# Sinkhorn attention followed by a routed expert layer: the first-layer tile's second bank no longer ordered behind the first bank's relu, the attention's exponential issued a unit earlier, expert pieces ahead of the placing, the ranking spread over the Sinkhorn rounds and GpSimd

## The chip, the cores and the metric

The kernel runs on one core of a Trainium2 chip. The metric is device time in microseconds (us) for one launch. A core has five engines, each of which takes its own instructions in order: TensorE (PE, with PEld for its weight loads), VectorE (DVE), ScalarE (ACT), GpSimd (POOL) and SyncE (SP); semaphores order them among each other, and DMA queues move data beside them. TensorE's results go to PSUM, from where ScalarE or VectorE copy them to SBUF (an "eviction").

## The reference, cut to what matters

```python
def _attn_ref(q, k, v, sort_net):            # (4, 8, 768, 64), 8 blocks of 96
    P = sort_net                             # (4, 8, 8, 8)
    for _ in range(5):
        P = np.exp(P - np.max(P, axis=-1, keepdims=True))
        P = P / (np.sum(P, axis=-1, keepdims=True) + 1e-09)
        P = P / (np.sum(P, axis=-2, keepdims=True) + 1e-09)
    k_sorted = einsum('bhij,bhjcd->bhicd', P, k_b)    # the same for v
    attn = softmax(scale * q_b @ k_sb.T)     # inside each block of 96
    return attn @ v_sb

def _moe_ref(x, modality_id, w_gate, modality_bias, w1, w2):   # x: 3072 x 512
    logits = x @ w_gate + modality_bias[modality_id]
    e_idx = np.argmax(logits, axis=1)        # one of 8 experts for each row
    gate_w = softmax(logits)[row, e_idx]
    out[mask] = gate_w * (np.maximum(x[mask] @ w1[e], 0) @ w2[e])
```

The rows of x are the attention's output, heads side by side. The kernel assumes that each of the two modalities sends its rows to one expert, the one that its bias prefers, checks that on the chip, and has a slow path that recomputes everything where it does not hold. The slow path does not run with this data.

## The kernel before, in words

**Start.** GpSimd issues the loads of `v`, `k`, `q` (halves of the batch: g = 0, 1) and fills constants. Five Sinkhorn rounds (L224 to L242) alternate one exponential on ScalarE with five small VectorE operations; TensorE meanwhile runs 28 matmuls on the identity (`spin`). Then `make_bd` turns P into a block matrix, `rank_a` to `rank_e` compute for each row its place among the rows of its modality (`m_` the modality bits, `cumz` running counts, `dest` the row's place within a block's window, `off` the window's offset, `eI` the two experts), on VectorE and TensorE. `load_w` reads `eI` into a register and issues the experts' weights; they go to two homes, wA and wB. `sort_v` (8 chunks, tiles `va`) and `sort_k` (6 chunks, tiles `ka`) mix the blocks by P; each chunk is evicted by ScalarE or VectorE, as `pick` decides from running sums of estimated cost. `prep_q` transposes q (tiles `tq`).

**Units.** There are 32 units, one for a pair of batches, a block and half of the heads: `scores(u)` (8 matmuls, tile `sc`), `expo(u)` (one exponential, 96x768, on ScalarE into `attnT[u % 2]`), `av(u)` (8 matmuls, tile `op`, then a reciprocal and a multiplication on VectorE into `xb`). Two units make a pair of blocks, and `place(t)` multiplies its 2 x 96 rows by the permutation `perm` into tile `pm` (10 matmuls) and copies them into the window of `XT` that `off` names: two copies on ScalarE for an even pair, on VectorE for an odd one. Rows of modality 0 gather from the front of `XT`, rows of modality 1 from its end.

**Slots and pieces.** `SLOTS` (L60) cuts `XT` into stretches of 128 or 256 rows, each with a home of weights and the number of pairs that have to be placed first. A slot is worked off in pieces: the gate `mG` (tile `lg`), the first layer `mL1` (tile `hp`, two PSUM banks, 4096 matmul columns; each bank is evicted by its own `relu` into `hT`), the second layer `mL2` (tile `yp`, 4096 columns, one eviction into `y` and one scattering DMA to `out`). `run_pieces(n)` takes the next n pieces whose slot's pairs are placed. There are 25 pieces of each layer.

**Order.** A manual schedule keeps every engine's instructions in the order in which the code emits them. PSUM tiles with two banks (`sc`, `op`, `pm`, `hp`, `va`, `ka`, `rk`) come from a pool of three, in turn, so that the fourth waits until the first has been evicted; `tq`, `lg` and `yp` come from a pool of two single banks. `do_unit` is the period of the units:

```python
def do_unit(u, last, n):
    expo(u)
    if u < last:
        scores(u + 1)
    if u % 2 == 0 and pending:
        do_place()
    run_pieces(n)
    av(u)
```

Units 0 to 6 of the first half run no pieces. Between the halves stand `sort_v(1)` and `sort_k(1)` with one piece behind each chunk, then eight `prep_q`. What is left of the pieces runs after the last unit; ahead of the last slot's second layer a check of the assumption runs on VectorE, and its one matmul (`gp`) stands in TensorE's order.

Of the kernel before, what the change touches and what calls it, by code (L numbers as in the profile page):

```python
# [24 lines left out]
def kernel(  # L25
# [15 lines left out]
    NB = 8  # L41
# [18 lines left out]
    SLOTS = [("A", 0, 256, 3), ("A", 256, 256, 6), ("B", 0, 256, 3), ("B", 256, 256, 6),  # L60
# [41 lines left out]
    v_in = singles.tile([128, 128, D], BF16)  # L102
# [84 lines left out]
    nc.gpsimd.memset(v_in[:, BLK:].rearrange("p c d -> p (c d)").bitcast(U32), 0)  # L187
# [8 lines left out]
    idm = singles.tile([BLK, 32, 128], BF16)  # L196
    nc.gpsimd.memset(idm.bitcast(U32), 0)
# [4 lines left out]
    nc.gpsimd.tensor_copy(idm[:, :, 0:2].rearrange("p o z -> p z o"), idI)  # L202
# [3 lines left out]
    nc.gpsimd.memset(XT[:, :, PAD0:CAP - PAD0].bitcast(U32), 0)  # L206
# [14 lines left out]
    for _ in range(28):  # L221
        nc.tensor.matmul(spin[:, 0].rearrange("p (a b) -> p a b", a=4), ident, id4, start=True, stop=True)

    for it in range(5):  # L224
# [4 lines left out]
        if it == 0:  # L229
            nc.vector.tensor_reduce(jmask, id3s, AX.X, ALU.add)  # L230
        elif it == 1:
            nc.vector.tensor_reduce(bmask, id3, AX.X, ALU.add)
        elif it < 4:
            nc.vector.tensor_copy(sel[it - 2], ident[0:BH, (it - 2) * 16:(it - 1) * 16].broadcast_to([BH, 16, NB]))
# [23 lines left out]
    def sort_v(g, ch):  # L258
        acc = ps(f"va{g}_{ch}").rearrange("p b (z x) -> p (b z) x", x=128)
        for z in range(8):  # L260
            nc.tensor.matmul(acc[:, z], v_in[:, :, ch * 8 + z], bd[g], start=True, stop=True)  # L261
        evac(v_sb[0:BLK, :, ch * 8:(ch + 1) * 8], acc[0:BLK].rearrange("p z x -> p x z"), 1024)
# [24 lines left out]
    st = {}  # L287

    def small(name, n, dt=FP32, rows=128):
        return singles.tile([rows, n], dt, tag=name, name=name)  # L290

    def rank_a():
        mbf = singles.tile([32, 3, 32], BF16)
        nc.vector.tensor_copy(mbf, modI[:, :, 0].rearrange("p (r t) -> p t r", t=3))
        mp = ps1("mp", BF16)[0:BLK, 0:32]
        nc.tensor.transpose(mp, mbf.rearrange("p t r -> p (t r)"), ident[0:32, 0:32])
        m_ = st["m"] = small("m_", 32, BF16, BLK)
        nc.vector.tensor_copy(m_.rearrange("p (g i r) -> p g i r", g=2, i=8),
                              mp.rearrange("p (g r i) -> p g i r", g=2, r=2))
        ci = st["ci"] = small("ci", 32, BF16, BLK)  # L300
        nc.vector.tensor_tensor_scan(ci, ones_bf[0:BLK, 0:32], m_, 0.0, ALU.mult, ALU.add)

    def rank_b():
        rk = st["rk"] = ps("rk")
        nc.tensor.matmul(rk[:, 1, 0:32], ones_bf[0:BLK], st["ci"], start=True, stop=True)
        nc.tensor.matmul(rk[:, 0, 0:32], maskUT[0:BLK], st["m"], start=True, stop=True)
        nc.vector.tensor_copy(cumz[:, 1:33], rk[:, 1, 0:32])
        f_ = st["f"] = small("f_", 1)
        nc.vector.tensor_scalar(f_, cumz[:, 32:33], float(HALF), None, ALU.is_le)
        d_ = small("d_", E)  # L310
        nc.vector.tensor_tensor(d_, bias2[:, 1], bias2[:, 0], ALU.subtract)
        bAB = st["bAB"] = singles.tile([128, 2, E], FP32, tag="bAB", name="bAB")
        nc.vector.scalar_tensor_tensor(bAB[:, 0], d_, f_, bias2[:, 0], ALU.mult, ALU.add)
        nc.vector.scalar_tensor_tensor(d_, d_, f_, bias2[:, 1], ALU.mult, ALU.subtract)
        nc.vector.tensor_scalar(bAB[:, 1], d_, -1.0, None, ALU.mult)
# [14 lines left out]
    def rank_ok():  # L330
        nm = st["nm"] = small("nm", 32)
        nc.vector.tensor_tensor(nm, cumz[:, 1:33], cumz[:, 0:32], ALU.subtract)
        w_ = small("w_", 33)
        nc.vector.tensor_tensor(w_, cumz, mid, ALU.subtract)
        dv = small("dv", 64)
        nc.vector.tensor_tensor(dv[:, 0:32], w_[:, 1:33], w_[:, 1:33], ALU.mult)
        nc.vector.tensor_scalar(dv[:, 32:64], nm, float(BLK // 2), None, ALU.subtract)
        nc.vector.tensor_tensor(dv[:, 32:64], dv[:, 32:64], dv[:, 32:64], ALU.mult)
        nc.vector.tensor_tensor(dv, dv, marg, ALU.is_le)
        good = st["good"] = small("good", 1)  # L340
        nc.vector.tensor_reduce(good, dv, AX.X, ALU.min)
# [540 lines left out]
```

## Time and profile before

| | |
|---|---|
| median of 3 runs | 258.31 us (257.79 to 259.61) |
| the profiled execution's own time | 259.06 us |
| its span in the trace | 257.3 us |
| TensorE matmul busy | 183.6 us (71%) |
| VectorE busy | 109.7 us (43%) |
| ScalarE busy | 93.3 us (36%) |
| GpSimd busy | 58.6 us (23%) |
| mean granted TensorE clock | 0.839 of 2.4 GHz |

The granted clock has two levels, 1.2 and 2.4 GHz (0.5 and 1.0 in the rows); a mean between them says for what share of a stretch each was granted. Matmul ends are modelled, so the step from one start to the next says more about a matmul's cost than the duration of a single row does.

### The profile page before, as it was taken

How to read it: one execution, taken by the hardware profiler on the slowest of the kernel's cores; microseconds unless marked ns; L12 is line 12 of the kernel's file. 1: busy time of each engine (PE TensorE's matmuls, PEld its weight loads, DVE VectorE, ACT ScalarE, POOL GpSimd, SP SyncE). 2: the span in 40 equal slices, each digit the busy share in tenths (PEclk: the TensorE clock that was granted, in tenths of full speed). 3: DMA queues.
4: the chain of work that ended last, by engine and by line, in shares of the span. 5: the costliest groups of instructions: out<-in, count | busy, mean ns of one | idle time of the engine just before them, and what ended most of it. 6: DMA issues, size and time to landing. Idle time of an engine off the chain costs nothing. (4 is left out here: it accounts for less than half of the span.)

```text
span 257.3 us, 5170 instructions
## 1 busy us (share of the span) xinstructions
PE 183.6 (71%) x2166; PEld 127.6 (50%) x2183; DVE 109.7 (43%) x294; ACT 93.3 (36%) x141; POOL 58.6 (23%) x102
## 2 busy tenths in 40 slices
PE   4756886568658778888987567676778747878581
PEld 1345765446435456676565345553555534555240
DVE  4878877750453272323435433325234460022411
ACT  2124466323632534334346414334434503433030
POOL 7877332100000157111310001011011111123013
PEclk9956675557855899999999659799799997999889
DMA  5999999998000119811111001011011110212101
GB/s 69 199 214 197 207 197 209 212 214 179 3 1 3 41 45 166 160 41 43 43 43 43 0 3 41 3 41 41 3 41 43 41 41 0 84 42 83 44 33 55
DMA packets 16460, 20.36 MB, mean 79 GB/s; under 512 B 9999, under 2 KB 12079, under 8 KB 16432
## 3 DMA queue, kind: packets, MB, share of 16 engines
q0 software_dynamic: 15664, 19.93, 39.0%
q8 instruction: 18, 0.29, 0.5%
q1 hardware_dynamic: 768, 0.06, 0.3%
q14 instruction: 10, 0.08, 0.1%
HBM read 27.32 MB, written 6.55 MB: 132 GB/s over the span
## 5 line engine op out<-in xcount | busy, mean ns | idle before, releaser
L547 POOL DMA_INDIRECT out_dram<-y,ids x25 | 24.5, 979 | 174.5 <-ACT y L544 131.3
L528 PE MATMUL hp<-XT,wA 128*128 128x256 bf16 (+1 forms) x224 | 32.7, 305 | 8.8 <-ACT hT L516 6.5
L528 PE MATMUL hp<-XT,wB 128*128 128x256 bf16 (+1 forms) x224 | 28.2, 272 | 11.5 <-ACT hT L516 6.1
L516 ACT ACTIVATE hT<-hp 128x512 bf16<-128x512 f32 x34 | 20.2, 595 | 36.7 <-PE hp L528 36.6
L539 PEld LDWEIGHTS <-hT 128*128 128x128 bf16 x200 | 19.4, 102 | 24.2 <-issue 6.7
L528 PEld LDWEIGHTS <-wA 128*128 128x128 bf16 x224 | 22.2, 113 | 17.0 <-issue 11.3
L528 PEld LDWEIGHTS <-wB 128*128 128x128 bf16 x224 | 20.5, 100 | 17.3 <-issue 14.0
L544 ACT ACTIVATE y<-yp,gate 128x512 f32<-128x512 f32 x16 | 11.0, 688 | 44.7 <-PE yp L539 44.7
L420 ACT ACTIVATE attnT<-sc 96x768 bf16<-96x768 f32 x32 | 24.9, 802 | 3.4 <-PE sc L414 3.4
L518 DVE TENSOR_SCALAR hT<-hp 128x512 bf16<-128x512 f32 x16 | 11.0, 689 | 34.3 <-PE hp L528 34.3
L539 PE MATMUL yp<-wA,hT 128*128 128x512 bf16 x87 | 24.1, 418 | 0.9 <-issue 0.6
L539 PE MATMUL yp<-wB,hT 128*128 128x512 bf16 x96 | 23.1, 382 | 0.9 <-issue 0.7
L435 DVE TENSOR_TENSOR xb<-op,rs_all 96x512 bf16<-96x512 f32 x32 | 22.0, 687 | 1.1
L430 PE MATMUL op<-v_sb,attnT 96*128 96x65 bf16 x256 | 15.8, 213 | 6.7 <-ACT attnT L420 6.7
L434 DVE RECIPROCAL rs_all<-op 96x8 f32<-96x8 f32 x32 | 6.4, 201 | 32.5 <-PE op L430 32.3
L459 PE MATMUL pm<-perm,xb 96*128 96x96 bf16 x128 | 13.3, 236 | 8.9 <-DVE xb L435 7.8
L430 PEld LDWEIGHTS <-attnT 96*128 96x128 bf16 x256 | 13.5, 111 | 10.9 <-ACT attnT L420 7.2
L414 PE MATMUL sc<-qT,kT 64*128 64x96 bf16 x256 | 12.8, 229 | 6.3 <-DVE xb L435 3.7
L471 DVE CAST XT<-pm 128x720 f32 x16 | 14.5, 909 | 6.1 <-PE pm L461 5.7
L546 DVE TENSOR_SCALAR y<-yp,gate 128x512 f32<-128x512 f32 x9 | 6.8, 751 | 23.4 <-PE yp L539 23.4
L261 PE MATMUL va<-bd,v_in 128*128 128x128 bf16 x128 | 14.4, 277 | 2.9 <-ACT v_sb L95 2.4
L471 ACT CAST XT<-pm 128x720 f32 x16 | 12.3, 768 | 10.4 <-PE pm L461 10.1
(142 smaller groups left out, 216.9 us busy)
## 6 DMA issues: line engine op xcount, KB each, us to landing
v_in<-in_v_dram POOLq DMA_DIRECT2D x8, 384.0 KB, 12.1
k_in<-in_k_dram POOLq DMA_DIRECT2D x6, 512.0 KB, 15.7
q_in<-in_q_dram POOLq DMA_DIRECT2D x16, 192.0 KB, 10.8
wA<-in_moe_w_dram POOLq DMA_DIRECT2D x4, 512.0 KB, 12.1
wB<-in_moe_w_dram POOLq DMA_DIRECT2D x4, 512.0 KB, 13.9
out_dram<-y,ids POOLq DMA_INDIRECT x25, 2.7
modI<-in_moe_modality_id_dram SPq DMA_DIRECT2D x1, 24.0 KB, 1.7
P_t<-in_sort_net_dram SPq DMA_DIRECT2D x1, 8.0 KB, 1.6
```

The source lines that it names most:

```text
L261: nc.tensor.matmul(acc[:, z], v_in[:, :, ch * 8 + z], bd[g], start=True, stop=True)
L414: nc.tensor.matmul(sc[:, r, j * BLK:(j + 1) * BLK].rearrange("p (t r) -> p t r", t=3), kT[rows, x0:x0 + 128], qT5[rows, i // 4, h, :, i % ...
L420: nc.scalar.activation(attnT[u % 2][:, 0:8 * BLK].rearrange("p (r f) -> p r f", r=2), sc_tiles.pop(u)[0:BLK, :, 0:4 * BLK], ACT.Exp, scale ...
L430: nc.tensor.matmul(op[:, r, j * (D + 1):(j + 1) * (D + 1)], attnT[u % 2][:, c0:c0 + 128], v_sb[0:BLK, r * 64 + (hh * 4 + j) * 8 + i, 0:D + ...
L435: nc.vector.tensor_tensor(xb[t % XB][:, :, hh * 256:(hh + 1) * 256].rearrange("p r (j d) -> p r j d", j=4), o4[:, :, :, 0:D], rs_all[:, u] ...
L459: nc.tensor.matmul(pm[:, r, c * BLK:(c + 1) * BLK], xt[:, r, c * 128:(c + 1) * 128], perm[:, o], start=True, stop=True)
L471: ins = (nc.scalar.copy if side(t) == "act" else nc.vector.tensor_copy)(d, s_).ins
L516: nc.scalar.activation(dst, src, ACT.Relu)
L518: nc.vector.tensor_scalar(dst, src, 0.0, None, ALU.max)
L528: mm = nc.tensor.matmul(hp[:, f], w1_t[m][:, c, fc * 128:(fc + 1) * 128], XT[:, c, row:row + n], start=(c == 0), stop=(c == 3))
L539: nc.tensor.matmul(yp, hT[s % 2][:, f, z * 128:(z + 1) * 128], w2_t[m][:, f], start=(f == 0), stop=(f == 7))
L547: ins = nc.gpsimd.indirect_dma_start(out=out, out_offset=bass.IndirectOffsetOnAxis(ap=ids[:, k_:k_ + 1], axis=0), in_=y, in_offset=None, b ...
```

## The change

Seven edits go together.

1. **Second bank.** In `mL1` the matmuls into the tile's second bank are declared independent of the relu that reads its first bank. In the built order the first of them waited for ScalarE or VectorE; now none of the second half has such a wait.
2. **Exponential a unit ahead.** `do_unit` issues `scores(u + 1)` and at once `expo(u + 1)`; before, it issued `expo(u)` at the head of unit u.
3. **Pieces ahead of placing.** In `do_unit` the pieces stand ahead of `do_place`, and a placing counts for the slots one unit later (`ready`). Units take two pieces where u is a multiple of 4, else one, from the first unit on; the slot list begins with two slots of 128 rows at 2 and 3 pairs and has 15 slots in place of 14 (still 25 pieces of each layer).
4. **Neighbouring work.** Four `prep_q` of each half stand between units in place of in one block; `sort_k(1)` comes ahead of `sort_v(1)`, with a piece behind every second chunk; `make_bd(1)` comes behind `sort_k(0)`.
5. **Ranks in the Sinkhorn rounds.** What was `rank_a` and the head of `rank_b` (modality bits, transpose, running count, two matmuls) stands inside the rounds, its copies on ScalarE; the 28 `spin` matmuls are spread as 10, 10 and 8 around its matmuls. Its PSUM tile is a single bank, copied at once.
6. **Ranks on GpSimd.** The arithmetic of `rank_b`, the squares of `rank_ok`, `rank_d` and `rank_e` moves from VectorE to GpSimd; the arg-max over experts (`rank_c`) and the thresholds (`rank_off`) stay on VectorE.
7. **Smaller constants.** `v_in` has 96 columns in place of 128 and needs no zero fill, so `sort_v` loads 96 weight columns; `idm` shrinks from 32 x 128 to 192 columns; the zero fill of `XT` is cut into five.

```diff
-    SLOTS = [("A", 0, 256, 3), ("A", 256, 256, 6), ("B", 0, 256, 3), ("B", 256, 256, 6),
+    SLOTS = [("A", 0, 128, 2), ("A", 128, 128, 3), ("B", 0, 256, 3), ("A", 256, 256, 6), ("B", 256, 256, 6),
...
+            spins(10)
         elif it == 1:
             nc.vector.tensor_reduce(bmask, id3, AX.X, ALU.add)
...
+            nc.scalar.copy(mbf, modI[:, :, 0].rearrange("p (r t) -> p t r", t=3))
+            nc.tensor.transpose(mp, mbf.rearrange("p t r -> p (t r)"), ident[0:32, 0:32])
+            spins(10)
...
+        elif it == 3:
+            nc.vector.tensor_tensor_scan(ci, ones_bf[0:BLK, 0:32], m_, 0.0, ALU.mult, ALU.add)
+            nc.tensor.matmul(rk[:, 32:64], ones_bf[0:BLK], ci, start=True, stop=True)
+            nc.tensor.matmul(rk[:, 0:32], maskUT[0:BLK], m_, start=True, stop=True)
+            spins(8)
+        else:
+            nc.scalar.copy(cumz[:, 1:33], rk[:, 32:64])
+            nc.scalar.copy(exr, rk[0:BLK, 0:32])
...
+                    if b:
+                        tc.declare_no_dep(mm.ins, group=grp, reason="the other bank of the tile is read")
             fs = slice(b * nf // 2, (b + 1) * nf // 2)
-            relu(hT[s % 2][:, half * 4 + b * nf // 2:half * 4 + (b + 1) * nf // 2, 0:n], hp[:, fs], 512)
+            ins = relu(hT[s % 2][:, half * 4 + b * nf // 2:half * 4 + (b + 1) * nf // 2, 0:n], hp[:, fs], 512)
+            tc.add_to_no_dep_group(grp, ins.ins)
...
+    def do_unit(u, last, n):
+        if u < last:
+            scores(u + 1)
+            expo(u + 1)
+        run_pieces(n)
+        if ready:
+            pairs[0] = ready.pop()
+        if u % 2 == 0 and pending:
+            do_place()
+        av(u)
+        if u % 2:
+            pending.append(u // 2)
+
+    for u in range(16):
+        do_unit(u, 15 if u != 7 else 8, 1 if u % 4 else 2)
+        if u in (1, 3, 5):
+            rank_p(u // 2 + 1)
+        if u in (3, 4, 5, 6):
+            prep_q(0, 1, u - 3)
...
+    for u in range(16, 32):
+        do_unit(u, 31, 1 if u % 4 else 2)
+        if 17 <= u < 21:
+            prep_q(1, 1, u - 17)
```

**ScalarE among the units.** `attnT0`/`attnT1` are the exponentials' outputs, `hT` the relus', `XT` a placing's copies, `y` a second-layer eviction. Before, around the placing of pair 4:

```order
L471 COPY XT_82<-pm4_1138 128x5x2x72 [waits Activation_49]
L420 ACTIVATE attnT1_78<-sc11_1124 96x768
L420 ACTIVATE attnT0_77<-sc12_1163 96x768 [waits PE_49]
L508 ACTIVATE es_all_94<-la_all_93 128x16 [waits DVE_49]
L516 ACTIVATE hT1_85<-hp1_0_1228 128x512 [waits PE_49]
L420 ACTIVATE attnT1_78<-sc13_1184 96x768 [waits Activation_49]
L544 ACTIVATE y0_86<-yp0_0_1268,gate_95 128x512 [waits PE_49]
```

Now, around the same placing:

```order
L437 ACTIVATE attnT0_77<-sc10_1161 96x768 [waits PE_49,Activation_49]
L525 ACTIVATE es_all_94<-la_all_93 128x16 [waits DVE_49]
L533 ACTIVATE hT0_84<-hp2_0_1188 128x512 [waits PE_49] x2
L437 ACTIVATE attnT1_78<-sc11_1218 96x768 [waits PE_49,Activation_49]
L564 ACTIVATE y1_87<-yp1_0_1228,gate_95 128x512 [waits PE_49]
L464 TENSOR_LOAD off_411
L488 ISA
L488 COPY XT_82<-pm4_1246 128x5x2x72 [waits PE_49]
```

The exponential of unit 11 stood behind the copies of pair 4; now it stands ahead of them and ahead of the unit's second-layer eviction.

**GpSimd at the start.** The load of the first expert's weights (`wA`) stood right behind the constants:

```order
L204 MEMSET wgp_167 128x90
L206 MEMSET XT_82 128x5x264
L393 TENSOR_LOAD eI_294 [waits DVE_49]
L393 ISA x2
L396 ISA
L396 DMA wA_66<-in_moe_w1_dram 128x2x1024 [waits DMASW3_49]
```

Now 19 rows of rank arithmetic stand between, of which these are the last four:

```order
L384 TENSOR_TENSOR d1_327<-d1_327,exr_186 96x32 [waits Pool_49]
L385 TENSOR_TENSOR d1_327<-d1_327,d0_322 96x32 [waits Pool_49]
L386 TENSOR_TENSOR d1_327<-d1_327,m__183 96x32 [waits Pool_49]
L388 TENSOR_TENSOR dest_332<-d1_327,d0_322 96x32 [waits Pool_49]
L410 TENSOR_LOAD eI_310 [waits DVE_49]
L410 ISA x2
L413 ISA
L413 DMA wA_66<-in_moe_w1_dram 128x2x1024 [waits DMASW3_49]
```

The load is issued behind them, still ahead of the second half of q and of `wB`.

**VectorE behind the block matrix.** Before, the ranking followed `bd0`, and the first eviction (`v_sb`) came 16 rows later; the first six rows:

```order
L255 TENSOR_TENSOR bd0_253<-bmask_171,rr0_251 128x128 [waits DVE_49]
L294 CAST mbf_255<-modI_107 32x96 [waits DMAHW1_49]
L298 COPY m__259<-mp_257 96x32 [waits PE_49]
L301 SCALAR_TENSOR_TENSOR ci_261<-ones_bf_118,m__259 96x32 [waits DVE_49,Pool_49]
L307 COPY cumz_144<-rk_263 128x32 [waits PE_49]
L309 TENSOR_SCALAR f__267<-cumz_144 128x1 [waits DVE_49]
```

Now:

```order
L284 TENSOR_TENSOR bd0_271<-bmask_175,rr0_269 128x128 [waits DVE_49]
L97 CAST v_sb_70<-va0_1_291 96x128x8 [waits PE_49]
L334 TENSOR_REDUCE mxb_301<-bAB_277 128x2 [waits Pool_49]
L335 TENSOR_TENSOR bAB_277<-bAB_277,mxb_301 128x16 [waits DVE_49]
L337 SCALAR_TENSOR_TENSOR keyb_304<-bAB_277,tie_124 128x16 [waits DVE_49]
```

An eviction comes first, and the arg-max that follows waits for GpSimd.

## Rows read from the trace of the kernel before

**Rows 1.** Busy time by stage: stretch, length, engines' busy us (instructions), clock, DMA share, GB/s

```profile
36.40:94.00 57.60, 40.23 (x476) 27.92 (x478) 26.51 (x57) 24.14 (x36) 6.20 (x10) 0.64 0.56 104
94.00:138.80 44.80, 38.16 (x578) 28.34 (x581) 17.57 (x38) 18.81 (x28) 13.18 (x16) 1.00 0.44 84
138.80:210.70 71.90, 48.06 (x543) 33.40 (x544) 29.26 (x69) 27.64 (x43) 6.77 (x7) 0.88 0.07 26
210.70:257.30 46.60, 32.74 (x232) 20.01 (x236) 8.78 (x35) 11.32 (x21) 8.73 (x9) 0.92 0.13 47
```

**Rows 2.** TensorE's waits, whole span: waiter, line, releaser: us, times, longest

```profile
PE hp L528 <- ACT hT L516: 12.6, 17, 1.0
...
PE op L430 <- ACT attnT L420: 6.7, 9, 1.9
PE hp L528 <- DVE hT L518: 6.6, 7, 1.6
...
PE gp L684 <- DVE gb L682: 2.9, 1, 2.9
```

**Rows 3.** Instructions in order of time, start to unit 8: start, us, engine, line, operation

```profile
8.82 1.49 DVE L234 COPY sel<-ident 32x128 bf16<-32x128 bf16 x1
...
14.11 0.29 DVE L255 TENSOR_TENSOR bd<-bmask,rr 128x128 bf16<-128x128 f32 x1
...
15.77 1.93 PE L261 MATMUL va<-bd,v_in 128*128 128x128 bf16 x16
...
16.88 1.02 ACT L95 CAST v_sb<-va 96x1024 bf16<-96x1024 f32 x1 [5.03 <-PE va L261]
...
18.95 1.21 DVE L97 CAST v_sb<-va 96x1024 bf16<-96x1024 f32 x1
...
36.43 1.50 ACT L420 ACTIVATE attnT<-sc 96x768 bf16<-96x768 f32 x2
...
54.47 0.45 PE L496 MATMUL lg<-wgp,XT 128*128 128x9 bf16 x10
```

**Rows 4.** GpSimd alone, in order of time, 16 to 21 us

```profile
16.15 0.46 POOL L202 CAST idm<-idI 96x64 bf16<-96x64 int32 x1
...
20.57 0.71 POOL L396 DMA_DIRECT2D wA<-in_moe_w_dram  x1 [2.74 <-DVE v_sb L97]
```

**Rows 5.** DMA issues by line: count, size of one, median us to landing

```profile
wA<-in_moe_w_dram POOLq DMA_DIRECT2D x4, 512.0 KB, 12.1
```

**Rows 6.** TensorE in order of time, 218 to 222 us, at clock 1.00

```profile
218.27 1.03 PE L528 MATMUL hp<-XT,wA 128*128 128x256 bf16 x8 [0.69 <-ACT hT L516]
219.14 1.89 PE L539 MATMUL yp<-wB,hT 128*128 128x512 bf16 x8
220.87 0.40 PE L496 MATMUL lg<-wgp,XT 128*128 128x9 bf16 x10
221.12 1.04 PE L528 MATMUL hp<-XT,wB 128*128 128x256 bf16 x8
```

**Rows 7.** TensorE in order of time, 85.4 to 88 us: one unit and one placing

```profile
85.45 0.46 PE L430 MATMUL op<-v_sb,attnT 96*128 96x65 bf16 x8
85.85 0.34 PE L414 MATMUL sc<-qT,kT 64*128 64x96 bf16 x8
86.94 0.34 PE L459 MATMUL pm<-perm,xb 96*128 96x96 bf16 x4 [0.75 <-DVE xb L435]
...
87.37 0.82 PE L528 MATMUL hp<-XT,wA 128*128 128x256 bf16 x6
```

**Rows 8.** One sorting chunk's weight loads, and two preparations of q

```profile
97.56 0.83 PEld L261 LDWEIGHTS <-v_in 128*128 128x128 bf16 x8
...
133.36 0.86 PE L283 MATMUL tq<-ident,q_in 128*64 128x128 bf16 x24
```

**Rows 9.** Instructions grouped by line: count, busy us, mean ns, idle before

```profile
L471 DVE CAST XT<-pm 128x720 f32 x16 | 14.5, 909 | 6.1 <-PE pm L461 5.7
```

**Rows 10.** TensorE's last matmuls, in order of time

```profile
248.36 3.40 PE L539 MATMUL yp<-wB,hT 128*128 128x512 bf16 x15
```

More of the change, by code (lines that the diff above doesn't have):

```diff
@@ L205 @@
     PAD0 = HALF - SPAN
-    nc.gpsimd.memset(XT[:, :, PAD0:CAP - PAD0].bitcast(U32), 0)
+    for c in range(5):
+        nc.gpsimd.memset(XT[:, c, PAD0:CAP - PAD0].bitcast(U32), 0)
     jmask = singles.tile([128, NB], FP32)
@@ L220, with spins, small @@
     id4 = bc_mid(ident, 4)
-    for _ in range(28):
-        nc.tensor.matmul(spin[:, 0].rearrange("p (a b) -> p a b", a=4), ident, id4, start=True, stop=True)
+    def spins(n):
+        for _ in range(n):
+            nc.tensor.matmul(spin[:, 0].rearrange("p (a b) -> p a b", a=4), ident, id4, start=True, stop=True)
+    st = {}
+    def small(name, n, dt=FP32, rows=128):
+        return singles.tile([rows, n], dt, tag=name, name=name)
+    mbf = singles.tile([32, 3, 32], BF16)
+    mp = ps1("mp", BF16)[0:BLK, 0:32]
+    m_ = st["m"] = small("m_", 32, BF16, BLK)
+    ci = st["ci"] = small("ci", 32, BF16, BLK)
+    rk = ps1("rk")
+    exr = st["ex"] = small("exr", 32, rows=BLK)
     for it in range(5):
@@ L460, in place @@
                                  start=True, stop=True)
-            nc.tensor.matmul(pm[:, r, 4 * BLK:5 * BLK], idm[:, o], perm[:, o], start=True, stop=True)
+            nc.tensor.matmul(pm[:, r, 4 * BLK:5 * BLK], idm[:, 2 * o:2 * o + 128], perm[:, o], start=True, stop=True)
         for r in range(2):
@@ L627, with do_place @@
         load_w("B", z)
+    for ch in range(2, 8):
+        sort_v(0, ch)
+        if ch == 4:
+            rank_off()
+    for ch in range(6):
+        sort_k(0, ch)
     for z in range(4):
         load_v(1, z)
-    for u in range(7):
-        do_unit(u, 7, 0)
-        if u in (1, 2, 3):
-            rank_p(u)
-    do_unit(7, 7, 0)
-    do_place()
-    run_pieces(2)
-    for hq in range(4):
-        prep_q(0, 1, hq)
-    scores(8)
     for z in range(3):
         load_k(1, z)
-    for u in range(8, 16):
-        do_unit(u, 15, 1)
-    do_place()
+    make_bd(1)
+    rank_p(0)
+    for hq in range(4):
+        prep_q(0, 0, hq)
+    scores(0)
+    expo(0)
+    pending, ready = [], []
+    def do_place():
+        t = pending.pop(0)
+        load_offs(t)
+        place(t)
+        ready.append(t + 1)
+    def do_unit(u, last, n):
[16 more added lines that the diff above has]
+            prep_q(0, 1, u - 3)
     for z in range(2):
```

212 lines of the change are left out of this document (88 added, 124 removed).

## The prediction, made before the changed kernel was timed

> **What bounds the kernel now.** I read three views in this order: the stages, TensorE's waits, and the rows at the places where the change cuts in. The stages [rows 1] show no engine that is full: TensorE, the busiest, works 40.23 of 57.60 us in the first units, 38.16 of 44.80 in the sorting between the halves, 48.06 of 71.90 in the second units and 32.74 of 46.60 at the end. ScalarE and VectorE stay near half, and the DMA share is small from 94 us on. Two things stretch TensorE's time. One is the clock: 0.64 and 0.88 in the two stages of units, against 1.00 in the sorting, where the gaps are shortest. The other is order: the waits [rows 2] are for work that TensorE started itself a moment earlier. The largest are the second bank behind the first bank's relu (12.6 + 6.6 us, 24 times, some 0.8 us each) and `av` behind its own exponential (6.7 us). So the bound is a chain of handovers, with a clock that falls where they are most frequent.
>
> **The change, part by part.** I price TensorE's work at 2.4 GHz by the step from one start to the next, add up the new order by stage, and add what still waits.
>
> *Prices.* Half a first-layer piece takes 0.87 us (218.27 to 219.14), so a piece 1.74; a second-layer piece 1.73; a gate 0.25 [rows 6]. One unit's `av` takes 0.40 and its scores 0.34, so 0.74 a unit; a placing 0.43 (86.94 to 87.37) [rows 7]. A sorting chunk takes 0.83 us, which its weight loads set; a preparation of q 0.43, half of 0.86 [rows 8]. As a test, the old tail by these prices: 16 pieces 27.8, 4 gates 1.0, 7 waits at second banks 5.4, the flag's matmul 2.9 [rows 2], 2.0 until the last placing's copies end, 5.5 from the last matmul's end (248.36 + 3.40) to the span's end [rows 10], in all 44.6 of 46.60 [rows 1]. The rest I put down to slow-clock work behind the flag's wait, and keep 1.5 of it below.
>
> *Start.* The first exponential now begins at 36.43 [rows 3]. A copy of `sel` took 1.49 us at 8.82 while GpSimd filled constants; it moves to ScalarE and the largest fill goes, so Sinkhorn ends some 0.9 us earlier. The block matrix is ready at 14.40 but the first sorting matmul starts at 15.77, behind the ranking: 1.37 us go. Together sorting starts near 13.5. Then 14 chunks are evicted, 8 on ScalarE at 1.02 us and 6 on VectorE at 1.21 us, and all three PSUM tiles are there from the beginning. VectorE sets the end: I let it wait for the counts that GpSimd now computes. GpSimd finishes its constants at about 16.7, needs five operations for the biases and five for the squares, and I take 0.25 us for each. Its own CAST of 96x64 took 0.46 [rows 4], which is my upper end; 0.1 is the lower. So the arg-max runs at 17.9 to 19.1, the thresholds at 20.3 to 22.4, and four more evictions of 1.21, the second block matrix, `perm` and the copies of q follow until scores can run: first exponential at 31.0, **5.4 us earlier**. The ends are 29.8 and 33.1. The weights for A are issued behind nine more GpSimd operations, near 21.3 in place of 20.57 [rows 4]; with 12.1 us to landing [rows 5] they are there by 36, and the first piece needs them at 44.5: hidden, with 8 us to spare. If that cover were gone, each us later would be a us on the path.
>
> *GpSimd against VectorE, the page that speaks against this.* The Trainium skill (SBUF — State Buffer, "SBUF: two separate sides") says that these two engines share a pair of ports which one instruction holds to its end while the other engine blocks. The 1.49 us of the `sel` copy agrees [rows 3], and by that rule each of the 19 moved operations could hold VectorE once: 19 x 0.25 = 4.8 us on its queue, the start at 35.8 in place of 31.0. Evictions went on at their usual length beside the fills, so I take none of it.
>
> *Units 0 to 15.* Units without pieces took (54.47 - 36.43) / 8 = 2.26 us each [rows 3]; VectorE and the three tiles pace them, and I leave that: units 0 to 5 take 13.5 us. Units 6 to 15 hold eight pieces (13.9), ten units (7.4), five placings (2.2), four gates (1.0) and a preparation (0.4): 24.9. The second bank and `av` no longer wait. What is late next is a placing's tile: with three tiles, the third allocation behind `pm` waits for the copies, 2 x 0.91 us on VectorE [rows 9], while only `av` and scores, 0.74, lie between. That is 1.1 us wherever no piece lies there: four times here, 4.4. The first piece and its placing run at the low clock, 2.5 more. Sum 45.3, ending at 76.3, with eight pieces done where before there were six at 94.
>
> *Sorting.* Eight pieces (13.9), 14 chunks (11.6), four preparations (1.7), a placing and two gates (0.9), waits 1.5: 29.6, ending at 105.9. The same prices give the old stage 22.6 + 11.6 + 3.4 + 1.0 + seven bank waits of 0.8 = 44.2 of 44.80 [rows 1].
>
> *Units 16 to 31.* Sixteen pieces (27.8), 16 units (11.8), seven placings (3.0), five gates (1.3), four preparations (1.7): 45.6. Units 18 to 21 have no pieces and keep their pace (3.5 more); one tile wait (1.1), the first exponential (0.9), low clock behind the bare units (2.5): 53.6, ending at 159.5.
>
> *Tail.* 18 pieces (31.2), placing and gates (1.4), the flag 2.9 and 1.5, the last relu 0.7, the end 5.5: 43.2. **Span 202.7.** The profiled execution has 259.06 beside a span of 257.3, so 204.5; the median of the runs is 0.75 below that execution, 203.7. Every handover also has a latency that I did not price, and the test sums came out 1 to 2 us low in a stage: 3 us more. **Forecast 207 us.** Its own range is 200 to 215: below, the start's lower end (1.2) and no tile waits (5.5); above, the start's upper end (2.1) and 0.4 us more at each of 16 placings.
>
> **Rivals.** *The units keep their waits (chance 0.20).* The second units lose 71.90 - 42 us of priced work today; I let them lose 8. If each of the 13 placings between units holds its tile until copies, reciprocal and multiplication have passed VectorE's queue, that is 1 us more at each, 220; the range is 215 to 232. For it speaks that three tiles serve scores, first layer, placing and `av`; against it that VectorE has 29.26 of 71.90 us busy [rows 1].
>
> *The second bank waits all the same (0.05).* If the relu is not what holds it, 19.2 us [rows 2] stay: 226. The built order no longer has the wait, which speaks against it.
>
> *GpSimd sets the start (0.08).* At 0.46 us for each of the ten operations that VectorE waits for [rows 4], 2.1 us are added, 209; with VectorE's queue held for 4.8 us as well, 214. The edge of this case is the 8 us that the weights have to spare.
>
> *The clock falls (0.07; of it 0.03 slower than now).* About 126 us of the new order are matmuls whose length follows the clock (50 pieces, 32 units, 16 placings, gates, preparations). My sum has 8 us of it at the low level, and each further us at 1.2 GHz costs one. With half of both unit stages at the low level the time is 234. It is slower than today, 262, when 62 of the 126 us run at 1.2 GHz; that needs tile waits so frequent that both unit stages stay below the 0.64 of the first one [rows 1]. The 1.00 of the sorting, with TensorE busy 38.16 of 44.80, speaks against it. The 0.88 of the second units shows that mixed clocks happen here.
>
> The Trainium skill (TensorE: Matmul & The Clock Gate, "A second HAM failure mode: psum-queue depth-cycling") describes a kernel whose TensorE idles briefly between groups as it cycles through PSUM banks, so that its clock swings between both levels. By that rule the new tile waits would bring this rival about; no run here shows it for waits as short as 1.1 us.
>
> *Better than summed (0.05).* If ScalarE's and VectorE's copies overlap so that no tile waits, 5.5 us go and the time is 196 to 200.
>
> **How the numbers follow.** The forecast has 0.55 and the rivals 0.20, 0.05, 0.08, 0.07 and 0.05. The predicted time is the likeliest case's. From 199 to 224 lie the forecast (0.55), the GpSimd case (0.08), some 0.13 of the units' case and half of the better one: 0.8 of the chance. A difference of about 1% is the least that a measurement of this kernel can tell from none. Faster by over 1% is every case but the worst of the clock and whatever I overlooked: 0.95; within 1% 0.02; slower 0.03.
>
> **What would show it.** Right: no wait of `hp` for a relu inside a piece; the first exponential near 31 us; the sorting near 76 to 106; granted clock near 1.0 from unit 8 on; waits of about 1 us for `XT` copies at the placings in their place. Wrong: `pm`, `op` or `sc` waiting 2 us and more for VectorE at every unit; a clock below 0.8 in units 22 to 31; a wait for wA at the first piece; or GpSimd's ranks longer than 0.5 us each.

## The result and the profile after

| | before | changed |
|---|---|---|
| median | 258.50 us (257.79 to 259.61, 4 runs) | 201.03 us (200.20 to 202.86, 4 runs) |
| ratio | | 0.778, 95% interval 0.772 to 0.785 |
| the profiled execution | 259.06 us, span 257.3 | 200.22 us, span 198.6 |

So 57.5 us went; the forecast was 207 us. Some runs of e3, e4, e5, f2 and f3 below were over 1.5% longer than the fastest of the same kernel, at a lower granted clock; the times given for these five kernels are the medians of their other runs. The stages of the changed kernel, cut at the first exponential, the first sorting matmul of the second half, the first exponential of that half and the last `av` (columns as in [rows 1]):

```profile
36.30:78.40 42.10, 35.28 (x534) 27.70 (x529) 26.77 (x64) 25.14 (x39) 6.58 (x10) 0.82 0.86 158
78.40:110.30 31.90, 31.12 (x455) 25.75 (x454) 14.07 (x24) 15.83 (x22) 10.72 (x13) 1.00 0.53 84
110.30:155.20 44.90, 41.90 (x603) 31.42 (x599) 26.67 (x69) 29.38 (x46) 7.24 (x8) 1.00 0.12 43
155.20:198.60 43.40, 34.95 (x288) 22.86 (x286) 13.78 (x44) 12.93 (x24) 10.81 (x11) 0.99 0.19 69
```

Against [rows 1], TensorE is now busy 31.12 of 31.90 us in the sorting and 41.90 of 44.90 in the second units, and its clock is 1.00 there. The largest waits of TensorE, as in [rows 2], behind the 3.4 us of the first `spin` for `ident`:

```profile
PE gp L702 <- DVE gb L700: 2.9, 1, 2.9
PE op L447 <- ACT attnT L437: 2.5, 3, 1.2
PE tq L312 <- DVE qT L97: 1.9, 1, 1.9
PE va L290 <- DMA v_in<-in_v_dram: 1.9, 1, 1.9
PE hp L545 <- ACT attnT L437: 1.6, 2, 1.0
```

No `hp` waits for a relu any more (19.2 us before). A first-layer piece answers to [rows 6] like this, TensorE in order of time:

```profile
161.36 1.91 PE L545 MATMUL hp<-XT,wA 128*128 128x256 bf16 x16
163.11 1.89 PE L559 MATMUL yp<-wB,hT 128*128 128x512 bf16 x8
164.83 1.91 PE L545 MATMUL hp<-XT,wA 128*128 128x256 bf16 x16
```

Both banks run on without a gap, 1.75 us from start to start; the second-layer piece takes 1.72. The start, however, did not get shorter. TensorE in order of time, against [rows 3]:

```profile
14.56 10.77 PE L290 MATMUL va<-bd,v_in 128*96 128x128 bf16 x64 [1.87 <-DMA v_in<-in_v_dram]
25.26 1.06 PE L302 MATMUL ka<-bd,k_in 64*64 64x64 bf16 x32
...
34.35 1.49 PE L312 MATMUL tq<-ident,q_in 128*64 128x128 bf16 x24 [1.94 <-DVE qT L97]
...
49.43 0.29 PE L513 MATMUL lg<-wgp,XT 128*128 128x9 bf16 x5
```

Eight chunks of `sort_v` took 10.70 us, 1.34 each, where the prediction used 0.83 [rows 8]. The first exponential began at 36.31, as before the change. The weight loads of the sorting, grouped by line, show it for both halves (13.6 us, 189 ns each, before); their columns lie 64 elements apart, and a load of 128 adjacent columns (the second line) takes 101 ns:

```profile
L290 PEld LDWEIGHTS <-v_in 128*96 128x96 bf16 x128 | 21.6, 257 | 3.2 <-issue 2.9
...
L545 PEld LDWEIGHTS <-wA 128*128 128x128 bf16 x256 | 20.1, 101 | 3.0 <-issue 1.3
```

GpSimd's ranks came as priced: the first at 16.30, the last at 22.01, 0.2 to 0.4 us each, and wA was issued behind them:

```profile
16.30 0.25 POOL L324 TENSOR_SCALAR f__273<-cumz 128x1 f32<-128x1 f32 x1
...
23.48 3.05 POOL L413 DMA_DIRECT2D wA<-in_moe_w_dram  x4 [1.23 <-issue]
```

### The profile page after: what moved, and what is told of

It is laid out like the page before. It is cut to its first block, busy times and chain, and to the rows that moved or that the text cites. A ratio compares the mean times of both kernels' runs of the same rounds, so it can differ in the third digit from the quotient of the medians.

```text
span 198.6 us, 5267 instructions
## 1 busy us (share of the span) xinstructions
PE 170.3 (86%) x2215; PEld 129.2 (65%) x2215; DVE 102.3 (52%) x266; ACT 95.8 (48%) x150; POOL 63.5 (32%) x133
## 4 chain that ended last, share of the span: by engine, by line
PE 75%; DVE 11%; DMA 5%; ACT 3%; issue 2%; POOL 1%; POOLq 0%; DVEq 0%; ACTq 0%
PE hp L545 23%; PE yp L559 22%; PE va L290 11%; DMA v_in<-in_v_dram 5%; PE op L447 5%; PE ka L302 4%; DVE xb L452 4%; PE pm L476 3%; PE sc L431 3%; PE tq L312 2%; DVE XT L488 2%; ACT attnT L437 2%; PE lg L513 1%; DVE rs_all L451 1%; ACT kT L95 1%
## 5 line engine op out<-in xcount | busy, mean ns | idle before, releaser
L559 PEld LDWEIGHTS <-hT 128*128 128x128 bf16 x200 | 18.7, 99 | 22.4 <-issue 3.4
L533 ACT ACTIVATE hT<-hp 128x512 bf16<-128x512 f32 x38 | 22.5, 595 | 15.3 <-PE hp L545 14.8
L545 PE MATMUL hp<-XT,wB 128*128 128x256 bf16 (+1 forms) x224 | 24.9, 265 | 1.4 <-DVE xb L452 0.7
L545 PE MATMUL hp<-XT,wA 128*128 128x128 bf16 (+1 forms) x256 | 23.8, 251 | 1.2 <-ACT attnT L437 1.0
L290 PEld LDWEIGHTS <-v_in 128*96 128x96 bf16 x128 | 21.6, 257 | 3.2 <-issue 2.9
L290 PE MATMUL va<-bd,v_in 128*96 128x128 bf16 x128 | 21.6, 346 | 1.9 <-DMA v_in<-in_v_dram 1.9
L545 PEld LDWEIGHTS <-wA 128*128 128x128 bf16 x256 | 20.1, 101 | 3.0 <-issue 1.3
L566 DVE TENSOR_SCALAR y<-yp,gate 128x512 f32<-128x512 f32 x11 | 8.3, 751 | 23.1 <-PE yp L559 23.1
L97 DVE CAST v_sb<-va 96x1024 bf16<-96x1024 f32 x8 | 9.8, 1219 | 13.9 <-PE va L290 13.9
L447 PEld LDWEIGHTS <-attnT 96*128 96x128 bf16 x256 | 11.9, 103 | 7.1 <-issue 2.1
L95 ACT CAST v_sb<-va 96x1024 bf16<-96x1024 f32 x8 | 8.1, 1008 | 15.9 <-PE va L290 15.9
```

The source lines that it names most:

```text
L95: nc.scalar.copy(dst, src)
L97: nc.vector.tensor_copy(dst, src)
L290: nc.tensor.matmul(acc[0:BLK, z], v_in[:, :, ch * 8 + z], bd[g], start=True, stop=True)
L447: nc.tensor.matmul(op[:, r, j * (D + 1):(j + 1) * (D + 1)], attnT[u % 2][:, c0:c0 + 128], v_sb[0:BLK, r * 64 + (hh * 4 + j) * 8 + i, 0:D + ...
L533: return nc.scalar.activation(dst, src, ACT.Relu)
L545: mm = nc.tensor.matmul(hp[:, f], w1_t[m][:, c, fc * 128:(fc + 1) * 128], XT[:, c, row:row + n], start=(c == 0), stop=(c == 3))
```

## The experiments

Each was timed together with the kernel before (258.7 to 259.4 us); where a difference is small, the intervals of the ratios to it are given.

| run | what it is | median us |
|---|---|---|
| e1 | before + edit 1 | 231.9 |
| e7 | before + edits 1 and 2 | 224.5 |
| g2 | before, `sort_v` with 96 columns | 266.4 |
| | the changed kernel | 201.0 |
| e2 | changed, edit 1 taken back | 228.4 |
| e4 | changed, edit 2 taken back | 217.2 |
| e5 | changed, placing ahead of the pieces | 208.8 |
| g1 | changed, a placed pair counts at once | 207.4 |
| e6 | changed, ranks on VectorE | 203.8 |
| e3 | changed, `v_in` 128 columns | 194.9 |
| f2 | e3, clearer start and later check | 190.7 |
| f3 | f2, q ahead of wA | 191.0 |

### e1: the kernel before with the first edit alone

```diff
                     reads(s, mm.ins)
+                    if b:
+                        tc.declare_no_dep(mm.ins, group=grp, reason="the other bank of the tile is read")
```

> The kernel before, with the first edit alone (second bank independent of the first bank's relu). By the sum of the prediction the 19.2 us of waits at second banks go and nothing else: 258.5 - 19.2 = 239 us. Rival one, the clock: these gaps also held the granted clock at 0.64 and 0.88 in the two stages of units; without them it rises and more goes than the waits, 225 to 233 us. Rival two, the wait moves on to the next handover (second layer behind the relu, or the placing's copies): 248 us or more.

Measured: 231.94 us, ratio 0.893 (0.886 to 0.900), 26.7 us less. The waits of `hp` for relus are gone, and the others stay, `av`'s at the same 6.7 us [rows 2]; the four longest in the units:

```profile
PE pm L459 <- DVE xb L435: 8.1, 14, 1.4
PE op L430 <- ACT attnT L420: 6.7, 9, 1.9
PE lg L496 <- DVE XT L471: 6.0, 3, 2.0
PE sc L414 <- DVE xb L435: 4.0, 6, 1.0
```

So the waits did not move on; the time lies in the clock rival's range, but the clock is only a part of it. The stage of the first units went from 57.4 us (sorting began at 93.81) to 50.1, with four first-layer pieces in it: by e2's price below 3.4 us are their waits, and the rest goes with the granted clock, 0.64 before [rows 1] and 0.73 here. The stage of the second units went from 67.5 us (first row, the kernel before, cut at the last `av`) to 59.7, with eight pieces, 6.8 us by that price, and there the clock did not rise (0.87 before, 0.86 here):

```profile
138.80:206.30 67.50, 47.02 (x525) 32.69 (x527) 25.89 (x64) 27.64 (x43) 5.80 (x6) 0.87 0.07 24
...
36.50:86.60 50.10, 35.38 (x474) 25.84 (x475) 26.39 (x57) 24.09 (x36) 6.00 (x10) 0.73 0.64 119
...
125.40:185.10 59.70, 46.18 (x524) 33.21 (x527) 25.79 (x64) 27.64 (x43) 5.80 (x6) 0.86 0.07 27
```

### e2: the changed kernel without the first edit

```diff
-                    if b:
-                        tc.declare_no_dep(mm.ins, group=grp, reason="the other bank of the tile is read")
...
-            tc.add_to_no_dep_group(grp, ins.ins)
```

> The changed kernel with the first edit taken back (the second bank waits for the first bank's relu again); all else as changed. By the sum: 25 first-layer pieces lose 0.8 us each, 201.0 + 20 = 221 us, clock still near 1.0 between 50 and 160 us. Rival one, the clock: with a gap in every piece the clock falls in the units as it did before, 235 us or more, with a granted clock of 0.9 or less there. Rival two, the denser order hides the relu already (the pieces stand ahead of other work): 205 us or less.

Measured: 228.43 us, ratio 0.880 (0.875 to 0.886), 27.4 us more than the changed kernel: between the sum and the clock rival. TensorE's waits name 19.6 us:

```profile
PE hp L545 <- ACT hT L533: 14.9, 19, 1.4
PE hp L545 <- DVE hT L534: 4.7, 6, 0.8
```

One piece in order of time shows why idle time is too low a price:

```profile
138.05 1.03 PE L545 MATMUL hp<-XT,wA 128*128 128x256 bf16 x8
139.77 1.03 PE L545 MATMUL hp<-XT,wA 128*128 128x256 bf16 x8 [0.68 <-ACT hT L533]
140.64 0.34 PE L476 MATMUL pm<-perm,xb 96*128 96x96 bf16 x4
```

From 138.05 to 140.64 are 2.59 us; the same piece of the changed kernel takes 1.74 (124.97 to 126.71). A wait shown as 0.68 costs 0.85: the matmuls ahead of it have to run out before the relu can start, 0.16 us that count as busy (a half takes 1.03 us as a row, 0.87 as a step). 25 pieces by 0.85 are 21.3 us. In the second units that is nearly all: 52.3 us in place of 44.9, 6.8 of the 7.4 for eight pieces, and the clock stays at 1.00 with a gap in each. In the first units and after the last `av` 4.1 and 3.0 us more are gone than the pieces' waits (8.4 and 9.8 us for five and eight pieces), and there the clock is lower: 0.76 against 0.82, 0.93 against 0.99. So the clock rival holds in places only.

### e3: 128 columns again

```diff
-    v_in = singles.tile([128, BLK, D], BF16)
+    v_in = singles.tile([128, 128, D], BF16)
...
+    nc.vector.memset(v_in[:, BLK:].rearrange("p c d -> p (c d)").bitcast(U32), 0)
     for it in range(5):
...
-            nc.tensor.matmul(acc[0:BLK, z], v_in[:, :, ch * 8 + z], bd[g], start=True, stop=True)
+            nc.tensor.matmul(acc[:, z], v_in[:, :, ch * 8 + z], bd[g], start=True, stop=True)
```

> The changed kernel with v_in 128 columns wide again; its 32 zero columns are filled by VectorE ahead of the Sinkhorn rounds (where it waits for the first load). Theory: a weight load of 96 columns is slower than one of 128. In the changed kernel 64 sorting matmuls took 10.70 us (0.167 each, in either half), before the change 16 took 1.66 us (0.104). So 8 chunks between the halves give back 8 x 0.50 = 4 us for certain, and of the 4 us in the first half some 2.5, until the evictions bound it: 194.5 us, weight loads 0.18 us instead of 0.26. Rival: the width is not the cause (the sorting is slower because of the order of its evictions, or the loads of other data beside it), and the time stays at 201 us. Second rival: the fill on VectorE delays Sinkhorn by its own length, 0.5 to 1 us, and the first half gains nothing: 197.5 us.

Measured: 194.91 us, 6.1 us less, ratio 0.756 (0.750 to 0.763) against 0.778 (0.772 to 0.785) of the changed kernel. The weight loads, and the first exponential on ScalarE:

```profile
L291 PEld LDWEIGHTS <-v_in 128*128 128x128 bf16 x128 | 12.7, 194 | 3.2 <-issue 2.9
```

```profile
31.54 0.81 ACT L438 ACTIVATE attnT<-sc 96x768 bf16<-96x768 f32 x1
```

The fill took 0.91 us from 1.14 on, before VectorE's first input had come, and delays nobody. The first exponential is 4.8 us earlier; the first gate only 3.2 us (46.22); 1.05 of the 1.6 us lost on the way are a new wait of TensorE for q's second half. The stage of the sorting is 28.9 us in place of 31.9. In the profiled executions 6.0 us went.

Not all of the start's 4.8 us is the load itself. From the first `sort_v` matmul to the first of `sort_k` are 7.36 us here (14.46 to 21.82) and 10.70 in the changed kernel, so 3.3 of the 4.8. Most of the rest comes behind it, where the granted clock is 1.00 here (22.0 to 31.5 us) and 0.66 there (25.3 to 36.3). The pace of the 96-column loads, however, does not go with the clock: a chunk took 1.34 us in the first half at 0.50, and 1.27 in the second at 1.00 (92.43 to 94.96 for two).

### g2: 96 columns in the kernel before

```diff
-            nc.tensor.matmul(acc[:, z], v_in[:, :, ch * 8 + z], bd[g], start=True, stop=True)
+            nc.tensor.matmul(acc[0:BLK, z], v_in[:, 0:BLK, ch * 8 + z], bd[g], start=True, stop=True)
```

> The kernel before with one edit alone: sort_v loads 96 of v_in's 128 columns (tile, zero fill and all else as before). Theory, 96 columns load slower (0.167 us a matmul in place of 0.104, as run e3 and the changed kernel show): the 8 chunks between the halves cost 8 x 0.5 = 4 us more and the 8 of the start, which partly wait for evictions, 2 to 3: 258.7 + 6.5 = 265 us. Rival: in e3 it was the fill on VectorE or the place of v_in in memory that helped, and not the width: 258.7 us. Rival: fewer columns are cheaper (96/128 of the load): 256 us.

Measured: 266.36 us, ratio 1.031 (1.025 to 1.037), 7.7 us more:

```profile
L261 PEld LDWEIGHTS <-v_in 128*96 128x96 bf16 x128 | 22.1, 256 | 2.7 <-issue 2.2
```

The first exponential moved from 36.43 to 39.20, and the stage between the halves from 45.0 to 49.0 us, as expected. Tile, fill and order are the same here, so the width alone does it.

### e4: the exponential in its old place

```diff
     def do_unit(u, last, n):
+        expo(u)
         if u < last:
             scores(u + 1)
-            expo(u + 1)
```

> The changed kernel with the second edit taken back: the exponential of unit u is issued at the head of unit u, behind the scores' matmuls of no other unit, instead of one unit earlier. By the prediction's step (av no longer waits for its own exponential, 6.7 us before): 201.0 + 6.7 = 207.7 us, with av waiting for attnT again some ten times. Rival: a piece or a placing stands between scores and av in most units, so the exponential is done in time in either order, and only the bare units lose: 201 to 203 us.

Measured: 217.22 us (216.13 and 218.31), 16.2 us more, above both theories. The waits are not where either looked:

```profile
PE sc L431 <- ACT attnT L437: 5.1, 5, 1.6
PE sc L431 <- DVE xb L452: 5.0, 6, 1.0
...
PE op L447 <- ACT attnT L437: 3.1, 6, 1.0
```

It is the *scores* that wait now, for an exponential or a multiplication that has still to free a tile: the three two-bank tiles go round, and an exponential that starts a unit later holds its tile a unit longer. The other part is the clock. The second units of e4 and of the changed kernel have 57.2 and 44.9 us, of which TensorE is idle 11.5 and 3.0 and busy 45.7 and 41.9. So 8.5 us are gaps and 3.8 are the same matmuls at a lower clock (0.91 against 1.00). The bare units show the change of level. In e4:

```profile
125.03 0.34 PE L431 MATMUL sc<-qT,kT 64*128 64x96 bf16 x8 [0.56 <-DVE xb L452]
125.93 0.62 PE L447 MATMUL op<-v_sb,attnT 96*128 96x65 bf16 x8 [0.56 <-ACT attnT L437]
...
131.50 0.51 PE L431 MATMUL sc<-qT,kT 64*128 64x96 bf16 x8 [1.60 <-ACT attnT L437]
```

In the changed kernel, the same units:

```profile
121.47 0.34 PE L476 MATMUL pm<-perm,xb 96*128 96x96 bf16 x4 [0.29 <-DVE xb L452]
...
124.08 0.42 PE L447 MATMUL op<-v_sb,attnT 96*128 96x65 bf16 x8 [1.04 <-DVE XT L488]
124.43 0.34 PE L431 MATMUL sc<-qT,kT 64*128 64x96 bf16 x8
```

In e4, after gaps of 0.70, 0.56 and 0.56 us, `av` takes 0.62 us in place of 0.42: the engine runs at 1.2 GHz (granted clock 0.50 from 126 to 136 us). With gaps of 0.29, 0.29 and 1.04 it stays at 2.4. It looks like the swing that the Trainium skill (TensorE: Matmul & The Clock Gate, "A second HAM failure mode: psum-queue depth-cycling") describes for a kernel that cycles through PSUM tiles. The trace of e4 agrees (0.91 in the second units); in the changed kernel, with a wait of 1.0 us, it does not occur (1.00).

### e7: the kernel before with edits 1 and 2

```diff
-        expo(u)
         if u < last:
             scores(u + 1)
+            expo(u + 1)
```

> The kernel before with two edits: the second bank independent (run e1, 231.9 us) and the exponential issued a unit ahead. Theory, waits alone: av's waits for its own exponential (6.7 us in e1, 9 times) go: 225 us. Rival, by run e4: the exponential is worth some 18 us wherever pieces stand among the units, because it also stands ahead of relus and copies on ScalarE: 214 us. Rival: in the order of before the bare units 0 to 7 are paced by the three tiles, and the exponential ahead takes the next scores' tile earlier, so nothing changes: 230 us or more.

Measured: 224.50 us, ratio 0.866 (0.862 to 0.869), 7.4 us below e1, as the theory has it, with the clock as in e1 (0.85 in both). But not all of it is `av`'s wait for its own exponential, which fell by 4.3 of the 6.7 us, to this:

```profile
PE op L430 <- ACT attnT L420: 2.4, 4, 1.0
```

The scores' wait for `xb` fell too, from 4.0 to 1.4 us, and a wait of `av` for `xb` is new (1.9 us). So the same edit is worth 7.4 us in the old order and 16.2 in the new one. That pieces among all units leave the tiles no slack there is my reading of e4's waits; no run shows it alone.

### e5 and g1: the two halves of the third edit

```diff
-        run_pieces(n)
-        if ready:
-            pairs[0] = ready.pop()
         if u % 2 == 0 and pending:
             do_place()
+            run_pieces(n)
+        else:
+            run_pieces(n)
+            if ready:
+                pairs[0] = ready.pop()
```

> The changed kernel with the order of half of the third edit taken back: in each even unit the placing is issued ahead of the unit's pieces again; which pairs count for the slots, and so which piece stands in which unit, stays. Theory one, the sum: each of the 13 placings between units then waits for the multiplication into xb of the unit before it, 0.75 us in the row of before and 0.16 us for the matmuls behind it that have run dry: 201.0 + 13 x 0.9 = 213 us. Rival, the relief is small: the scores of the next unit stand between, so the wait is 0.3 us: 205 us. Rival, clock: what run e4 showed (a reordering that takes away 10 us of waits moves the time by 18) holds here too, 219 us or more with a granted clock under 0.95 in the units.

Measured: 208.77 us, ratio 0.805 (0.799 to 0.811): 7.7 us more, between the first theory (213) and the small one (205).

```profile
PE pm L476 <- DVE xb L452: 5.4, 12, 0.6
```

Twelve placings wait, as the first theory has it, but 0.45 us each and not 0.75, and three do so in the changed kernel already (0.8 us). That is 4.6 us more, with 0.16 us of draining for nine more waits 6.0 of the 7.7 us. The profiled execution took 210.78 us; its clock is 0.78 in the first units and 0.93 in the second, where the changed kernel has 0.82 and 1.00, so the third theory holds in part, though not its 219 us.

```diff
         place(t)
         ready.append(t + 1)
+        pairs[0] = t + 1
```

> The changed kernel with the other half of the third edit taken back: a placed pair counts for the slots at once, not a unit later; the placing still stands behind the unit's pieces. Pieces then come up to a unit earlier, gates right behind the copies into XT that they read. Theory: gates wait for these copies as in run e1 (lg for XT 7.7 us, 4 times) and each wait empties TensorE: 201.0 + 6 to 9 = 207 to 210 us. Rival: with the placing behind the pieces, an av and the next scores always lie between, 0.74 us of the 1.8 us that the copies take, and half of the wait is left: 204 us. Rival: pieces that come earlier fill the bare units, and nothing is lost: 200 to 201 us.

Measured: 207.44 us, ratio 0.800 (0.796 to 0.804): 6.4 us more, the theory of the gates. They wait 5.3 us in six places; the changed kernel has no such wait:

```profile
PE lg L513 <- DVE XT L488: 2.8, 4, 1.1
PE lg L513 <- ACT XT L488: 2.5, 2, 1.4
```

### e6: the ranks on VectorE again

```diff
-        nc.gpsimd.tensor_scalar(f_, cumz[:, 32:33], float(HALF), None, ALU.is_le)
+        nc.vector.tensor_scalar(f_, cumz[:, 32:33], float(HALF), None, ALU.is_le)
...
```

(all of `fold`, `rank_b`, `rank_ok`, `rank_d` and `rank_e` likewise)

> The changed kernel with the arithmetic of the ranks on VectorE again (rank_b, rank_ok, rank_d, rank_e), at the same places of the order; the counts stay in the Sinkhorn rounds. Theory one: VectorE, which evicts 6 of the 14 first sorting chunks, gets some 24 operations of 0.15 to 0.36 us more before its second eviction, about 5 us, and the first exponential comes 3 to 5 us later: 204 to 206 us. Rival: in the changed kernel TensorE's 96-column loads set the pace of the sorting (its evictions wait for it, 1.6 us each), so VectorE has that time to spare: 201 to 202 us. Rival: GpSimd's longer operations and the later loads of wA cost more than they give, and it is faster, 199 us.

Measured: 203.84 us, ratio 0.786 (0.781 to 0.791), whose interval overlaps that of the changed kernel: 2.8 us more by the medians, not settled by the times. The first exponential came at 37.40, 1.1 us later. The slow sorting leaves VectorE most of the room, as the rival says; with 128 columns the edit may be worth more, which was not tried.

### f2 and f3: a version that beats both

f2 is e3 with `make_bd(1)` moved behind unit 7, the first `rank_p` behind unit 0, and the matmul of the check two pieces later:

```diff
-    make_bd(1)
-    rank_p(0)
...
-        if u in (1, 3, 5):
-            rank_p(u // 2 + 1)
+        if u in (0, 1, 3, 5):
+            rank_p((u + 1) // 2)
+        if u == 7:
+            make_bd(1)
...
+            st["gb"] = gb
+        elif "flag" in st and "nI" not in st and pieces and pieces[0][1] is mL2 and pieces[0][2] == (NS - 1, 0):
             gp = ps("gp")
```

> Run e3 (128 columns, 195.8 us) with two more steps: the second half's block matrix and the first perm leave the place ahead of q's evictions (VectorE's 0.72 and 0.95 us there; TensorE waited 1.9 us for q's copy), and the check's matmul, for which TensorE waited 2.93 us, is issued one second-layer and one first-layer piece later. Theory: 1.7 us at the start and 2.9 + 0.2 us at the end go: 191 us. Rival: the first units only wait longer for q's second half, which landed at 39 us in e3, and give the start's gain back: 192.7 us. Rival: the check's VectorE work then delays the last evictions, or its result comes after the last matmul, and the end keeps its 3 us: 194 us.

Measured: 190.67 us (190.66 and 190.67), too few for an interval. This is the theory's 191 by its number, but not by its sum. The end gave what was expected: from the last `av` to the span's end 40.1 us in place of 43.4, and the check's matmul waits for nobody:

```profile
179.89 0.17 PE L705 MATMUL gp<-gb,ones_bf 128*128 128x1 bf16 x1
```

The start did not: the first exponential came at 29.82, 1.7 us earlier than in e3, but the first gate at 46.66, 0.4 us later: the first rival's outcome, though TensorE's waits for q did not grow (0.91 us, 1.05 in e3). f3 moves the loads of q:

```diff
     rank_d()
+    for z in range(2):
+        for r in range(2):
+            load_q(0, 1, r, z)
     for z in range(4):
         load_w("A", z)
```

> Run f2 (two of its four times 190.7 us, two near 195) with one more step: the loads of q's second half are issued ahead of those of wA instead of behind them. In f2 TensorE waited 0.28 and 0.63 us for q at 38.6 and 39.2 us, and the first units took 16.8 us from the first exponential (29.8) to the first gate (46.7) where the changed kernel took 13.1. Theory: q lands some 8 us earlier and these units go back to 13 to 14 us: 187.5 to 188 us, and 64 columns of q hold nobody. Rival: the copies of perm and the exponentials set the pace there and only the two waits go: 189.5 us. Rival: wA comes some 3 us later and is now waited for at the first piece: 191 us or more.

Measured: 191.02 us (189.18 to 191.46, 4 runs), ratio 0.736 (0.732 to 0.741): below e3 and the changed kernel, not below f2. The waits for q are gone and the first gate is where it was, 46.61. In their place stands a gap for which the trace shows no cause:

```profile
33.69 0.22 PE L432 MATMUL sc<-qT,kT 64*128 64x96 bf16 x2 [2.74 <-issue]
```

f2 has it too (1.83 us). What it is stays open, and so do the 2 us at this place.

## Why the prediction was right, and where it was off

| | predicted | changed kernel | e3 (128 columns) |
|---|---|---|---|
| first exponential | 31.0 | 36.3 | 31.5 |
| first gate | 44.5 | 49.4 | 46.2 |
| second half's sorting begins | 76.3 | 78.4 | 75.4 |
| it ends | 105.9 | 110.3 | 104.3 |
| end of the units (last placing) | 159.5 | 157.2 | 151.2 |
| span | 202.7 | 198.6 | 192.6 |

**The start failed, through one step.** "A sorting chunk takes 0.83 us, which its weight loads set" was taken over from loads of 128 columns for loads of 96. Measured: 1.34 us. That cost 4.8 us at the start and 3 of the 31.9 in the sorting (e3, and g2 the other way round). I had let VectorE set the start's end; instead it waited for TensorE ahead of its second, fourth, fifth and sixth eviction (0.43, 1.05, 2.81 and 0.41 us). The rest of this step came near: sorting began at 14.56 (forecast 13.5; it waited for `v_in`), the arg-max ran at 18.6 to 19.7 (17.9 to 19.1), the thresholds to 23.2 (22.4), and wA was in time. With 128 columns the first exponential is at 31.5, half a microsecond from the forecast, though the sorting begins 1 us later than forecast there too. The Trainium skill has the rule that spoke against this edit and that I did not weigh (TensorE: Matmul & The Clock Gate, "Weight-path perf modes — Fast Weight Load (FWL) and DoubleRow"): the fast weight load is on when there are 128 weights that are not FP32. The traces agree: 194 ns with 128 columns, 257 with 96. By the rule of the Trainium skill on the same page ("LDWEIGHTS") that a load's time goes with its columns, 96 columns would be the cheaper ones; measured, they are not.

**GpSimd.** The 35.8 us that I had named for a start in which each of the 19 moved operations holds VectorE once looked right by its number alone (36.3). That is not the cause: e3 has the same 19 operations on GpSimd, and the start there is 31.5.

**Units 0 to 15** took 42.1 us, 3.2 less than priced. TensorE's waits among units 6 to 15 have the size that I priced (0.2 to 1.0 us, 4.1 in all against 4.4), but that is luck: I had charged them to the copies into `XT` behind each placing, and none of the seven is for those. They are for `xb` (2.4 us), `attnT` (1.6) and `hT` (0.2); the one wait for `XT` copies, 1.04 us, stands in unit 21. The low clock cost less than the 2.5 us that I charged: the first piece took 2.56 us in place of 1.78, and from 52 us on the clock is 1.00.

**Sorting**: 31.9 against 29.6, the loads again; 28.9 in e3. One error hid another: I had priced all 14 chunks at 0.83 us, but the six of `sort_k` took 0.57 each (78.38 to 79.51 for two), 1.6 us less in all.

**Units 16 to 31**: 46.9 against 53.6. I had charged 8.0 us above the prices of the work (pace of the bare units, a tile wait, the first exponential, low clock). Units 18 to 21 took 7.3 us (117.17 to 124.43) where their work is 5.6 by the prices, and the clock stayed at 1.00.

**Tail**: 41.4 against 43.2. The 3 us for unpriced handovers were not needed.

So the errors went both ways: +7.6 us in start and sorting, -11.7 in units and tail. What held of the mechanism is the main part of it: no first-layer piece waits for its own relu, the pieces fill the units, and the clock is near 1.00 from 52 us on. The range of the forecast (200 to 215) had the time, but that the sum of 202.7 lies so near the span of 198.6 is partly luck, since the errors cancel. Two sizes in its reasoning were wrong beside the loads. A wait at a second bank costs 0.16 us of drain beside the idle time that I counted, and takes the clock with it in places, so the first edit is worth 27 us (e1, e2) and not 19.2. And "`av` no longer waits" described the second edit too narrowly: what it gives in the new order is above all the scores' tile and the clock behind it, 16.2 us (e4).

**Of the rivals**, "the units keep their waits" (220) did not happen; e4 (217) and e5 (209) show what it looks like when the second edit or the placing's order is missing. "The second bank waits all the same" would have been 228 (e2), not 226. The clock did not fall; in e4 it did, for 10 us in the second units.

**What each edit gave.** In order: the first 26.7 us, the second 7.4, the others together 23.5 (224.5 to 201.0). Taken back alone, the placing's order costs 7.7, its lag 6.4, the ranks 2.8 (not clear of the noise), and the columns gain 6.1; that leaves some 13 us for the preparations between units, the ranks in the Sinkhorn rounds, the order of the sorting and what they do together, which I did not take apart.

## What to carry to other kernels

Price a wait by the step from start to start with and without it, not by its idle time, and count the clock that it takes along in places: 19.2 us of shown waits were worth 27. With few PSUM tiles in turn, ask which work frees a tile, and when; here an edit that frees it a unit earlier was worth 7.4 us in the old order and 16.2 in the new one. And do not price a trimmed weight load by the row of the full one: the same operation at another shape needs its own row. Here, with columns 64 elements apart, padding to 128 was the faster way.

## What the hardware showed that I had not expected

- A bf16 weight load of 96 columns that lie 64 elements apart takes 257 ns and one of 128 such columns 194 ns (189 in the kernel before), on the mean over both halves; 128 adjacent columns take 101 ns. With its matmul of 128 columns the step is 0.167 us against 0.104; 8 chunks of 8 matmuls cost 4.0 us more where TensorE is the bound (g2).
- TensorE fell to 1.2 GHz after three gaps of 0.56 to 0.70 us among bare units (e4, granted clock 0.50 from 126 to 136 us), and did not with a gap of 0.7 to 1.1 us in every first-layer piece of the second units (e2).
- Operations of 1 to 64 columns took 0.18 to 0.42 us on GpSimd and mostly 0.14 to 0.36 on VectorE (in the kernel before one took 1.03 us at 16.82), and VectorE's evictions beside them kept their 1.22 us.
